# Agent attention with a gated FFN: the score passes regrouped by row half, one finished column per block

## The chip, the cores and the metric

One core of a Trainium2 chip runs the kernel; the other cores are idle. The metric is the device time of one execution in microseconds (us). Three executions of the kernel before took 1880.52, 1881.68 and 1882.74 us, median 1881.68 us. One further execution was profiled and took 1880.13 us.

## The reference

For four batches of 12480 tokens with 128 channels and 49 agents per batch, cut to what matters:

```python
a2k     = softmax(scale * agents @ k.T)        # 49 x 12480, per batch
agent_v = a2k @ v                              # 49 x 128
q2a     = softmax(scale * q @ agents.T)        # 12480 x 49
x       = q2a @ agent_v                        # 12480 x 128
h       = x @ w_in                             # 128 -> 2048
out     = (h * sigmoid(1.702 * h)) @ w_out     # 2048 -> 128
```

The scores `agents @ k.T` and `q @ agents.T` are what the change is about. The FFN on 49920 tokens is the bulk of the arithmetic.

## The kernel before

**The array in halves.** TensorE works as two row halves: a matmul takes 64 rows of its operands (rows 0 to 63 for half 0, 64 to 127 for half 1), and a matmul of half 0 and one of half 1 run side by side, each into a PSUM bank of its own. The FFN does this in `up` (bank `ph`) and `down` (bank pair `po`) through the helper `on_rows`, so line 119 stands for all these matmuls. An operand in full precision is kept as a high and a low part, and three products (high by high, high by low, low by high) make one. The low part `gl` of an activation is made on VectorE by `low` (line 611), from `g` and its high part `gh`; `gh` comes from a DMA that converts, or from a cast on ScalarE (line 605).

**Groups.** One key group is 8 blocks of 120 tokens, one query group 8 blocks of 128 tokens. A group's tile has channels on the partitions and tokens along the row. `split` takes it apart into three bf16 parts x0, x1, x2 by four pieces on VectorE: pieces 0 and 1 (line 228, then 230) make x1 and x2 of the first half of the columns, pieces 2 and 3 those of the second half. x0 is the upper half of each word and needs no work.

**Scores.** `scores` takes the eight blocks in turn. Channels 0 to 63 lie on row half 0 and channels 64 to 127 on row half 1, so each half computes a partial score of the same block by six bf16 products, and half k leaves its partial sum in bank k of a pair `ps_m`. Eight blocks, six products, two halves: 96 matmuls a group (line 243). `score_sum` adds the two partial sums: ScalarE copies bank 0 to SBUF (line 255), and VectorE adds bank 1 to the copy (line 256). For keys the sum goes to `score`. For queries it goes to `e_sb`, and `query_shift` then takes the maximum over the agents (line 528) and subtracts it (line 529). There are 39 key groups (batches 1 to 3; batch 0 goes another way at the start, through `first_scores`) and 49 query groups.

**Order.** The order on every engine is written out by hand: a step counter t advances by two, each pair of steps does `up`, `low`, `high` and `down` for two feature tiles, and a table `at[t]` says which attention job goes into which step. The keys of batch 1 are placed by `K_FIRST` every four steps (13 groups, some 100 to 240 us into the span); those of batches 2 and 3 by `K_AT`, at wider spacing. The bank pair of scores, of the query transposes and of the key-value products is one buffer (`ps_m`, one at a time), so a user of the pair waits until the one before has been read out. VectorE, ScalarE and TensorE each take their instructions strictly in the order written.

**Loads.** A key group comes by one DMA on the SyncE queue (line 261), 13 steps ahead, into one of three buffers; the agents come by one DMA at the very start (line 122), ahead of the first queries (line 519).

Of the kernel before, what the change touches and what calls it, by code (L numbers as in the profile page):

```python
# [8 lines left out]
F32 = mybir.dt.float32  # L9
F32R = mybir.dt.float32r  # L10
BF16 = mybir.dt.bfloat16
# [4 lines left out]
ALU = mybir.AluOpType  # L16
AX = mybir.AxisListType

P = 128
TB = 120  # L20
KB = 8
KG = TB * KB
QB = 128
CH = 512
# [25 lines left out]
def kernel(  # L50
# [10 lines left out]
    nc = tc.nc  # L61
    B, C, N = qT.shape
    A = agT.shape[2]
# [6 lines left out]
    H = P // 2  # L70
# [33 lines left out]
    def two_banks():  # L104
        return turns[1].tile([P, 2, 512], F32, name="ps_m", tag="pair")
# [94 lines left out]
    ag_part = odd.tile([P, B, 3, A], BF16, name="ag_part")  # L200

    def split_agents():
        rest = ag_sb
        for i in range(3):
            nc.vector.tensor_copy(out=ag_part[:, :, i, :], in_=rest)
            if i < 2:
                ag_rest = work.tile([P, B, A], F32, name="ag_rest")
                nc.vector.tensor_sub(out=ag_rest, in0=rest, in1=ag_part[:, :, i, :])
                rest = ag_rest

    def halves(t):
# [21 lines left out]

    def scores(parts, places, ps=None):
        x0, x1, x2 = parts
        ps = bank_pair(ps)
        products = [(x0, 0), (x0, 1), (x0, 2), (x1, 0), (x1, 1), (x2, 0)]
        for j, parts in enumerate(places):
            for b, t0, o, n in parts:
                for i, (x, y) in enumerate(products):  # L240
                    for k in range(2):
                        r = rows(k)
                        nc.tensor.matmul(  # L243
                            out=ps[k][o : o + n, j * A : (j + 1) * A],
                            lhsT=x[r, t0 : t0 + n],
                            rhs=ag_part[r, b, y, :],
                            start=(i == 0),
                            stop=(i == len(products) - 1),
                            tile_position=(k * H, o),
                        )  # L250
# [12 lines left out]

    def first_keys(g):
# [247 lines left out]
    def query_load(n):  # L512
        t = loads.tile([P, GT], F32, name="qt", tag="qt", bufs=1)
        for c in range(2):
            m = 2 * n + c
            for lo in range(0, CH, width(m)):
                for b, i, j in spans(m * CH, width(m)):
                    t0 = m * CH + i - b * N
                    nc.sync.dma_start(
                        out=t[:, c * CH + lo + i : c * CH + lo + j], in_=qT[b, :, t0 : t0 + j - i]  # L520
                    )
        return t

    def query_shift(ps):
        sd = e_sb[:QB, :, 0:A]
        score_sum(ps, QB, sd)
        m = work.tile([P, KB], F32, name="m")
        nc.vector.tensor_reduce(out=m[:QB], in_=sd, axis=AX.X, op=ALU.max)
        nc.vector.tensor_tensor(
            out=sd, in0=sd, in1=m[:QB].unsqueeze(2).broadcast_to([QB, KB, A]), op=ALU.subtract  # L530
        )
        return sd

# [147 lines left out]
            pieces[n](i)  # L681

    def do_key_scores(b, g):
        banks[b, g] = scores(k_parts.pop((b, g)), [[(b, j * TB, 0, P)] for j in range(KB)])
# [12 lines left out]
    def do_query_scores(n, ps=None):  # L697
        if n < NG:
            places = []
            for j in range(KB):  # L700
                m = 2 * n + j * 2 // KB
                t0 = m * CH + j * QB % CH % width(m)
                places.append([(b, j * QB + lo, lo, hi - lo) for b, lo, hi in spans(t0, QB)])
            banks[n] = scores(q_parts.pop(n), places, ps)

    def do_query_shift(n):
# [36 lines left out]
    with tc.manual_schedule(engines={E.PE, E.Activation, E.DVE, E.Pool, E.SP}):  # L743
# [7 lines left out]
        nc.vector.tensor_copy(out=ag_0[:, 0:A], in_=ag_sb[:, 0, :])  # L751
        split_agents()
        for c in range(2):
            nc.vector.tensor_add(
# [284 lines left out]
```

## Time and profile before

| what | value |
|---|---|
| median of three executions | 1881.68 us |
| the profiled execution's own time | 1880.13 us |
| its span | 1878.4 us |
| TensorE matmul busy | 1852.3 us (99%) |
| VectorE busy | 1535.7 us (82%) |
| ScalarE busy | 1491.5 us (79%) |
| mean granted TensorE clock | 0.999 |

Busy time of TensorE is read with care: matmuls are pipelined, and the end of each is modelled, so a short pause may be hidden by the modelled end of the matmul before it. The span is 1.73 us shorter than the execution's own time, and that execution is 1.55 us below the median.

### The profile page before, as it was taken

The numbers are of one execution on the slowest core, as the hardware profiler recorded it, in microseconds if no ns is written. First come the engines' busy times: TensorE is split into PE (matmuls) and PEld (weight loads), VectorE is DVE, ScalarE is ACT, GpSimd is POOL, SyncE is SP. The second block draws the span as 40 slices with busy tenths as digits, with TensorE's granted clock in tenths as the row PEclk, the third lists the DMA queues.
The fourth block names the chain that finished last, engine by engine and source line by source line (L and its number), as shares of the span: only waits on it lengthen the run. The fifth ranks groups of instructions, "written<-read, shape, count | busy, mean of one in ns | idle before, by whom it ended". The sixth has DMA issues, their size and how long they took to land.

```text
span 1878.4 us, 56411 instructions
## 1 busy us (share of the span) xinstructions
PE 1852.3 (99%) x24100; PEld 1714.4 (91%) x24100; DVE 1535.7 (82%) x1978; ACT 1491.5 (79%) x2410; POOL 332.5 (18%) x591
## 2 busy tenths in 40 slices
PE   7999999999999999999999999999999999999999
PEld 4678889998899999899889999999989999999998
DVE  7888999888789899888778998998877677777765
ACT  3677787887778777888887877878878888888886
POOL 1111111111111111121111111111111121211111
PEclk9999999999999999999999999999999999999999
DMA  9577777777577777777757777777666666666665
GB/s 360 186 225 216 210 209 213 217 211 223 166 206 225 212 213 221 206 210 218 216 170 217 215 212 219 215 214 210 196 180 186 196 198 197 206 199 198 198 191 148
DMA packets 138108, 390.99 MB, mean 208 GB/s; under 512 B 16825, under 2 KB 18489, under 8 KB 137857
## 3 DMA queue, kind: packets, MB, share of 16 engines
q0 software_dynamic: 77776, 255.10, 47.6%
q1 hardware_dynamic: 60081, 132.29, 22.9%
q8 instruction: 189, 3.10, 0.7%
q14 instruction: 62, 0.51, 0.1%
HBM read 81.53 MB, written 50.99 MB: 71 GB/s over the span
## 4 chain that ended last, share of the span: by engine, by line
PE 88%; DVE 5%; DMA 3%; issue 2%; ACT 2%; SPq 0%; POOL 0%; POOLq 0%; DVEq 0%; ACTq 0%
PE po L119 53%; PE ph L119 26%; PE ps_m L243 5%; PE ps_m L119 2%; DVE gl L611 2%; DMA kt<-kT 1%; DMA gh<-g 1%; ACT g L593 1%; DVE rest L228 1%; PE ps_m L505 1%; DVE rest L230 1%; PE ps_m L559 1%; DMA outT<-o 1%; DMA words<-w_out 0%; PE ph L284 0%
## 5 line engine op out<-in xcount | busy, mean ns | idle before, releaser
L593 ACT ACTIVATE g<-ph 128x512 f32<-128x512 f32 x1568 | 807.8, 603 | 275.6 <-PE ph L119 263.7
L611 DVE TENSOR_TENSOR gl<-g,gh 128x1024 fp32r<-128x1024 f32 x776 | 922.1, 1213 | 73.6 <-ACT gh L605 51.6
L119 PE MATMUL po<-gh,wo_h 64*128 64x512 f32 (+1 forms) x3104 | 548.0, 395 | 0.1
L119 PE MATMUL po<-gl,wo_h 64*128 64x512 f32 (+1 forms) x3104 | 535.6, 387 | 3.1 <-DVE gl L611 2.8
L119 PE MATMUL po<-gh,wo_l 64*128 64x512 f32 (+1 forms) x3104 | 533.3, 386 | 0.0
L603 POOL DMA_DIRECT2D gh<-g x436 | 236.5, 544 | 1371.0 <-ACT g L593 1067.2
L119 PEld LDWEIGHTS po<-gl,wo_h 64*128 64x128 f32 x3104 | 365.1, 184 | 22.5 <-DVE gl L611 9.7
L119 PEld LDWEIGHTS po<-gh,wo_l 64*128 64x128 f32 x3104 | 367.0, 184 | 14.2 <-issue 0.2
L119 PE MATMUL ph<-hi,wh 64*128 64x512 f32 (+4 forms) x1616 | 373.8, 384 | 0.3 <-DVE wl L509 0.3
L119 PE MATMUL ph<-hi,wl 64*128 64x512 f32 (+4 forms) x1616 | 371.6, 381 | 0.0
L119 PE MATMUL ph<-lo,wh 64*128 64x512 f32 (+4 forms) x1616 | 370.8, 380 | 0.4 <-DMA lo<-lo 0.4
L605 ACT CAST gh<-g 128x1024 fp32r<-128x1024 f32 (+1 forms) x340 | 357.6, 1053 | 9.0
L119 PEld LDWEIGHTS po<-gh,wo_h 64*128 64x128 f32 x3104 | 348.5, 185 | 15.8 <-issue 4.6
L119 PEld LDWEIGHTS ph<-hi,wh 64*128 64x128 f32 x1616 | 208.2, 184 | 14.5 <-ACT g L593 5.7
L119 PEld LDWEIGHTS ph<-lo,wh 64*128 64x128 f32 x1616 | 208.5, 184 | 8.9 <-DMA lo<-lo 0.8
L119 PEld LDWEIGHTS ph<-hi,wl 64*128 64x128 f32 x1616 | 206.5, 184 | 7.2 <-issue 0.7
L638 ACT COPY o<-po 128x1024 f32<-128x1024 f32 x97 | 98.4, 1014 | 56.6 <-PE po L119 55.9
L230 DVE TENSOR_TENSOR rest<-rest 128x512 bf16<-128x512 f32 (+2 forms) x176 | 129.2, 741 | 0.9
L243 PE MATMUL ps_m<-ag_part,rest 64*128 64x49 bf16 x4188 | 119.8, 181 | 0.3 <-DVE rest L230 0.3
L243 PEld LDWEIGHTS <-rest 64*128 64x128 bf16 (+1 forms) x4236 | 112.3, 93 | 0.8 <-DVE rest L230 0.4
L644 POOL DMA_DIRECT2D outT<-o x97 | 85.3, 880 | 96.4 <-DMA outT<-o 70.2
L256 DVE TENSOR_TENSOR e_sb<-ps_m,e_sb 128x392 f32<-128x392 f32 x48 | 27.1, 565 | 89.5 <-ACT e_sb L255 89.5
(143 smaller groups left out, 1322.0 us busy)
## 6 DMA issues: line engine op xcount, KB each, us to landing
gh<-g POOLq DMA_DIRECT2D x434, 512.0 KB, 3.5
kt<-kT SPq DMA_DIRECT2D x52, 480.0 KB, 5.0
outT<-o SPq DMA_DIRECT2D x97, 256.0 KB, 2.0
outT<-o POOLq DMA_DIRECT2D x97, 256.0 KB, 4.2
qt<-qT SPq DMA_DIRECT2D x94, 256.0 KB, 4.9
vt<-v SPq DMA_DIRECT2D x39, 480.0 KB, 4.9
hi<-hi SPq DMA_DIRECT2D x96, 128.0 KB, 2.8
lo<-lo SPq DMA_DIRECT2D x96, 128.0 KB, 2.4
```

Source lines behind the costliest of these rows:

```text
L119: nc.tensor.matmul(out=out, lhsT=lhsT[r], rhs=rhs[r], start=start, stop=stop, tile_position=(k * H, 0))
L228: nc.vector.tensor_sub(out=r[:, s], in0=t[:, s], in1=halves(t)[0][:, s])
L230: nc.vector.tensor_sub(out=halves(r)[1][:, s], in0=r[:, s], in1=halves(r)[0][:, s])
L243: nc.tensor.matmul(out=ps[k][o : o + n, j * A : (j + 1) * A], lhsT=x[r, t0 : t0 + n], rhs=ag_part[r, b, y, :], start=(i == 0), stop=(i == ...
L256: nc.vector.tensor_add(out=out, in0=h[1], in1=out)
L505: nc.tensor.matmul(out=pw[:, i * 256 : i * 256 + m], lhsT=w["avT"], rhs=w_in_sb[:, t : t + m], start=True, stop=True)
L593: nc.scalar.activation(out=g[:, k, :n], in_=ph[k][:, :n], func=AF.Gelu_apprx_sigmoid)
L603: nc.gpsimd.dma_start(out=gh, in_=g)
L605: nc.scalar.copy(out=gh, in_=g)
L611: nc.vector.tensor_sub(out=gl, in0=g, in1=gh.bitcast(F32))
L638: nc.scalar.copy(out=o, in_=po[:, :, :n])
L644: nc.gpsimd.dma_start(out=outT[:, m * CH : m * CH + width(m)], in_=o[:, 1], accum_op=ALU.add)
```

## The change

Each row half gets four blocks of its own (half 0 blocks 0 to 3, half 1 blocks 4 to 7) and takes both channel halves of them in turn, six products each. So twelve products accumulate into one column range, and a score is finished in PSUM; nothing is left to add. For that the tiles are laid out otherwise: rows 0 to 63 hold the first four blocks, with channels 0 to 63 in the first half of the columns and channels 64 to 127 in the second; rows 64 to 127 hold the last four blocks in the same way. The agents are kept twice, once on each row half.

The score copy of a key group is one ScalarE instruction, and the addition is gone. A query group has neither copy nor addition: the maximum and the subtraction read PSUM. A key load is two DMAs of 64 partitions, and so is the load of the agents; the query loads stay two DMAs, each of 64 partitions now. The core of the diff:

```diff
-    ag_sb = odd.tile([P, B, A], F32, name="ag_sb")
-    nc.sync.dma_start(out=ag_sb, in_=agT)
+    ag_sb = lines.tile([P, 2, B, A], F32, name="ag_sb", tag="o", bufs=1)
+    for k in range(2):
+        nc.sync.dma_start(out=ag_sb[rows(k)], in_=agT.rearrange("(h p) b a -> p h b a", h=2))
...
     def scores(parts, places, ps=None):
         x0, x1, x2 = parts
-        ps = bank_pair(ps)
-        products = [(x0, 0), (x0, 1), (x0, 2), (x1, 0), (x1, 1), (x2, 0)]
-        for j, parts in enumerate(places):
-            for b, t0, o, n in parts:
-                for i, (x, y) in enumerate(products):
+        ps = two_banks() if ps is None else ps
+        products = [(h, x, y) for h in range(2) for x, y in ((x0, 0), (x0, 1), (x0, 2), (x1, 0), (x1, 1), (x2, 0))]
+        half = KB // 2
+        for j in range(half):
+            blocks = [places[j], places[half + j]]
+            for piece in range(max(len(x) for x in blocks)):
+                for i, (h, x, y) in enumerate(products):
                     for k in range(2):
...
+                                out=ps[o : o + n, k, j * A : (j + 1) * A],
+                                lhsT=x[rows(k), h * half * t0[1] + t0[0] : h * half * t0[1] + t0[0] + n],
+                                rhs=ag_part[rows(k), h, b, y, :],
...
-    def score_sum(ps, n, out):
-        h = [ps[k][:n, : KB * A].rearrange("p (j a) -> p j a", a=A) for k in range(2)]
-        nc.scalar.copy(out=out, in_=h[0])
-        nc.vector.tensor_add(out=out, in0=h[1], in1=out)
+    def blocks_of(ps, n):
+        return ps[:n, :, : KB // 2 * A].rearrange("p k (j a) -> p k j a", a=A)
...
     def key_load(b, g):
         t = loads.tile([P, KG + PAD], F32, name="kt", tag="kv")
-        nc.sync.dma_start(out=t[:, 0:KG], in_=kT[b, :, g * KB : (g + 1) * KB, :].rearrange("p j t -> p (j t)"))
+        for k in range(2):
+            j = g * KB + k * KB // 2
+            nc.sync.dma_start(
+                out=t[rows(k), 0:KG].rearrange("p (h x) -> p h x", h=2),
+                in_=kT[b, :, j : j + KB // 2, :].rearrange("(h p) j t -> p h (j t)", h=2),
+            )
...
     def query_shift(ps):
+        s = blocks_of(ps, QB)
         sd = e_sb[:QB, :, 0:A]
-        score_sum(ps, QB, sd)
         m = work.tile([P, KB], F32, name="m")
-        nc.vector.tensor_reduce(out=m[:QB], in_=sd, axis=AX.X, op=ALU.max)
+        mk = m[:QB].rearrange("p (k j) -> p k j", k=2)
+        nc.vector.tensor_reduce(out=mk, in_=s, axis=AX.X, op=ALU.max)
...
     def do_key_store(b, g):
-        score_sum(banks.pop((b, g)), TB, score[:TB, g * KB : (g + 1) * KB, :])
+        out = score[:TB, g * KB : (g + 1) * KB, :].rearrange("p (k j) a -> p k j a", k=2)
+        nc.scalar.copy(out=out, in_=blocks_of(banks.pop((b, g)), TB))
```

Besides, the split of the agents into three bf16 parts (`split_agents`) runs over 392 elements a row instead of 196, and the agents of batch 0 are copied by two instructions of 64 partitions.

Two places show how the order moves. The first is VectorE among the keys of batch 1, before; each row is a line of the kernel, an operation, output and inputs, the output's size and in brackets the engines it waits for. `kt` is a key tile, `rest` the low parts of a split, `score` and `e_sb` the scores of keys and queries, `gl` the low part of an activation:

```order
L256 TENSOR_TENSOR e_sb<-ps_m,e_sb 128x8x49 [waits Activation_49]
L528 TENSOR_REDUCE m<-e_sb 128x8 [waits DVE_49]
L529 TENSOR_TENSOR e_sb<-e_sb,m 128x8x49 [waits DVE_49]
L611 TENSOR_TENSOR gl<-g,gh 128x1024
L256 TENSOR_TENSOR score<-ps_m,score 120x392 [waits Activation_49]
L228 TENSOR_TENSOR rest<-kt 128x488 [waits DMAHW4_49]
L611 TENSOR_TENSOR gl<-g,gh 128x1024 [waits DMASW7_49]
L414 TENSOR_TENSOR run_max<-score,run_max 120x392 [waits DVE_49]
```

The same place in the changed kernel, whose line numbers are higher by 1 to 12:

```order
L537 TENSOR_REDUCE m<-ps_m 128x8 [waits PE_49]
L538 TENSOR_TENSOR e_sb<-ps_m,m 128x8x49 [waits DVE_49]
L623 TENSOR_TENSOR gl<-g,gh 128x1024 [waits Activation_49]
L229 TENSOR_TENSOR rest<-kt 128x488 [waits DMAHW1_49,DMAHW0_49]
L623 TENSOR_TENSOR gl<-g,gh 128x1024 [waits DMASW7_49,PE_49]
L421 TENSOR_TENSOR run_max<-score,run_max 120x392 [waits Activation_49]
```

Both additions (line 256) are gone; the query's maximum waits for TensorE instead of ScalarE, and the wait for ScalarE's copy of the key scores has moved behind the split and the next low part, to the running maximum.

The second place is the SyncE queue at the same stretch, before; `hi` and `lo` are parts of the weights of a query group, which change row halves there:

```order
L261 DMA kt<-kT 128x960 [waits DMAHW4_49,DVE_49,PE_49]
L577 DMA hi_1663<-hi 64x512 [waits DMASW1_49,DMAHW5_49,DMASW0_49,Activation_49]
L577 DMA hi_1663<-hi 64x512 [waits DMAHW6_49]
L577 DMA lo_1664<-lo 64x512 [waits DMASW3_49,DMAHW7_49,DMASW2_49,DVE_49]
L577 DMA lo_1664<-lo 64x512 [waits DMAHW0_49]
L261 DMA kt<-kT 128x960 [waits DMAHW1_49,DVE_49,PE_49]
```

And in the changed kernel:

```order
L265 DMA kt<-kT 64x2x480 [waits DMAHW0_49,DVE_49,PE_49]
L265 DMA kt<-kT 64x2x480 [waits DMAHW1_49]
L589 DMA hi_1662<-hi 64x512 [waits DMASW1_49,DMAHW2_49,DMASW0_49,Activation_49]
L589 DMA hi_1662<-hi 64x512 [waits DMAHW3_49]
L589 DMA lo_1663<-lo 64x512 [waits DMASW3_49,DMAHW4_49,DMASW2_49,DVE_49]
L589 DMA lo_1663<-lo 64x512 [waits DMAHW5_49]
L265 DMA kt<-kT 64x2x480 [waits DMAHW6_49,DVE_49,PE_49]
L265 DMA kt<-kT 64x2x480 [waits DMAHW7_49]
```

One issue more stands in the queue for every key group, ahead of what follows it; the order is otherwise the same.

## Rows read from the trace of the kernel before

**Rows 1.** The page's first lines: span, busy time and instructions of each engine.

```profile
span 1878.4 us, 56411 instructions
PE 1852.3 (99%) x24100; PEld 1714.4 (91%) x24100; DVE 1535.7 (82%) x1978; ACT 1491.5 (79%) x2410; POOL 332.5 (18%) x591
```

**Rows 2.** Busy time by stretch: columns as in the head row.

```profile
core 0: us, PE busy (x) PEld busy (x) DVE busy (x) ACT busy (x) POOL busy (x), PEclk, DMA share, GB/s
6.00:50.00 44.00, 36.91 (x402) 22.99 (x404) 32.63 (x72) 19.04 (x45) 2.38 (x4) 0.96 1.02 388
...
100.00:240.00 140.00, 134.21 (x2530) 116.72 (x2527) 127.51 (x176) 105.34 (x170) 22.93 (x48) 1.00 0.73 214
...
400.00:1850.00 1450.00, 1449.24 (x18598) 1371.01 (x18596) 1176.31 (x1456) 1185.45 (x1893) 263.65 (x460) 1.00 0.71 205
```

**Rows 3.** Waits in 100 to 240 us: in total, times, longest.

```profile
DVE score L256 <- ACT score L255: 11.4, 4, 3.3
...
PE po L119 <- DVE gl L611: 2.6, 4, 1.0
PE ps_m L243 <- DVE e_sb L256: 2.4, 3, 1.2
```

**Rows 4.** Timeline of VectorE around a late key copy: start, us, instruction, idle before.

```profile
141.20 0.57 DVE L545 TENSOR_TENSOR p_pad<-e_sb,z 128x392 f32<-128x392 f32 x1
145.05 0.56 DVE L256 TENSOR_TENSOR score<-ps_m,score 120x392 f32<-120x392 f32 x1 [3.28 <-ACT score L255]
145.53 0.66 DVE L228 TENSOR_TENSOR rest<-kt 128x488 f32<-128x488 f32 x1
146.11 2.35 DVE L611 TENSOR_TENSOR gl<-g,gh 128x1024 fp32r<-128x1024 f32 x2
```

**Rows 5.** Timeline of GpSimd's queue and of TensorE, the same moment.

```profile
138.62 0.53 POOL L603 DMA_DIRECT2D gh<-g  x1 [0.44 <-DVE rest L228]
...
147.38 0.73 PE L119 MATMUL po<-gl,wo_h 64*128 64x512 f32 x4 [0.52 <-DVE gl L611]
```

**Rows 6.** Timeline of VectorE and TensorE up to a wait for the bank pair.

```profile
112.97 0.57 DVE L256 TENSOR_TENSOR score<-ps_m,score 120x392 f32<-120x392 f32 x1 [1.81 <-ACT score L255]
...
129.54 0.39 PE L119 MATMUL ph<-hi,wl 64*128 64x512 f32 x2
...
129.77 0.39 PE L119 MATMUL ph<-lo,wh 64*128 64x512 f32 x2
...
130.75 0.55 DVE L256 TENSOR_TENSOR e_sb<-ps_m,e_sb 128x392 f32<-128x392 f32 x1
...
131.35 0.25 PE L243 MATMUL ps_m<-ag_part,kt 64*128 64x49 bf16 x6 [1.20 <-DVE e_sb L256]
```

**Rows 7.** Groups of instructions by line: busy us, mean ns, idle before, releaser.

```profile
L529 DVE TENSOR_TENSOR e_sb<-e_sb,m 128x392 f32<-128x392 f32 x49 | 27.8, 567 | 1.7
...
L256 DVE TENSOR_TENSOR e_sb<-ps_m,e_sb 128x392 f32<-128x392 f32 x48 | 27.1, 565 | 89.5 <-ACT e_sb L255 89.5
...
L256 DVE TENSOR_TENSOR score<-ps_m,score 120x392 f32<-120x392 f32 x39 | 22.0, 563 | 45.3 <-ACT score L255 45.2
...
L297 DVE TENSOR_REDUCE first_mx<-ph 128x1 f32<-128x480 f32 x12 | 7.5, 652 | 4.9 <-PE ph L284 4.9
```

**Rows 8.** Timeline of VectorE and TensorE: a key split that ends inside its score group.

```profile
151.16 0.25 PE L243 MATMUL ps_m<-ag_part,kt 64*128 64x49 bf16 x6
151.25 0.23 PE L243 MATMUL ps_m<-ag_part,rest 64*128 64x49 bf16 x6
151.29 0.73 DVE L230 TENSOR_TENSOR rest<-rest 128x480 bf16<-128x480 f32 x1
```

**Rows 9.** Timeline of SyncE at the start, and one key load later.

```profile
0.75 0.39 SPq L122 DMA_DIRECT2D ag_sb<-agT  x1
...
120.51 0.34 SPq L261 DMA_DIRECT2D kt<-kT  x1
```

**Rows 10.** The page's DMA issues: count, KB each, median us to landing.

```profile
kt<-kT SPq DMA_DIRECT2D x52, 480.0 KB, 5.0
```

More of the change, by code (lines that the diff above doesn't have):

```diff
@@ L198, in down_weights_low @@
         nc.vector.tensor_sub(out=wo_l[:, s, :], in0=wo, in1=wo_h[:, s, :].bitcast(F32))
-    ag_part = odd.tile([P, B, 3, A], BF16, name="ag_part")
+    ag_part = odd.tile([P, 2, B, 3, A], BF16, name="ag_part")
     def split_agents():
@@ L204, in split_agents @@
         for i in range(3):
-            nc.vector.tensor_copy(out=ag_part[:, :, i, :], in_=rest)
+            nc.vector.tensor_copy(out=ag_part[:, :, :, i, :], in_=rest)
             if i < 2:
-                ag_rest = work.tile([P, B, A], F32, name="ag_rest")
-                nc.vector.tensor_sub(out=ag_rest, in0=rest, in1=ag_part[:, :, i, :])
+                ag_rest = lines.tile([P, 2, B, A], F32, name="ag_rest", tag="rest")
+                nc.vector.tensor_sub(out=ag_rest, in0=rest, in1=ag_part[:, :, :, i, :])
                 rest = ag_rest
@@ L235, in scores @@
         x0, x1, x2 = parts
-        ps = bank_pair(ps)
-        products = [(x0, 0), (x0, 1), (x0, 2), (x1, 0), (x1, 1), (x2, 0)]
-        for j, parts in enumerate(places):
-            for b, t0, o, n in parts:
-                for i, (x, y) in enumerate(products):
-                    for k in range(2):
[L242 to L250, printed above, removed]
@@ L251, in scores @@
-        return ps
-    def score_sum(ps, n, out):
-        h = [ps[k][:n, : KB * A].rearrange("p (j a) -> p j a", a=A) for k in range(2)]
-        nc.scalar.copy(out=out, in_=h[0])
-        nc.vector.tensor_add(out=out, in0=h[1], in1=out)
+        ps = two_banks() if ps is None else ps
[5 more added lines that the diff above has]
+                for i, (h, x, y) in enumerate(products):
+                    for k in range(2):
+                        if piece < len(blocks[k]):
+                            b, t0, o, n = blocks[k][piece]
+                            nc.tensor.matmul(
+                                out=ps[o : o + n, k, j * A : (j + 1) * A],
+                                lhsT=x[rows(k), h * half * t0[1] + t0[0] : h * half * t0[1] + t0[0] + n],
+                                rhs=ag_part[rows(k), h, b, y, :],
+                                start=(i == 0),
+                                stop=(i == len(products) - 1),
+                                tile_position=(k * H, o),
+                            )
@@ L259, in key_load @@
+        return ps
+    def blocks_of(ps, n):
+        return ps[:n, :, : KB // 2 * A].rearrange("p k (j a) -> p k j a", a=A)
     def key_load(b, g):
         t = loads.tile([P, KG + PAD], F32, name="kt", tag="kv")
[L261 removed]
+        for k in range(2):
[3 more added lines that the diff above has]
+                in_=kT[b, :, j : j + KB // 2, :].rearrange("(h p) j t -> p h (j t)", h=2),
+            )
@@ L519, in query_load @@
                     nc.sync.dma_start(
-                        out=t[:, c * CH + lo + i : c * CH + lo + j], in_=qT[b, :, t0 : t0 + j - i]
+                        out=t[rows(c)].rearrange("p (h x) -> p h x", h=2)[:, :, lo + i : lo + j],
+                        in_=qT[b, :, t0 : t0 + j - i].rearrange("(h p) t -> p h t", h=2),
                     )
@@ L524, in query_shift @@
     def query_shift(ps):
+        s = blocks_of(ps, QB)
         sd = e_sb[:QB, :, 0:A]
-        score_sum(ps, QB, sd)
         m = work.tile([P, KB], F32, name="m")
-        nc.vector.tensor_reduce(out=m[:QB], in_=sd, axis=AX.X, op=ALU.max)
+        mk = m[:QB].rearrange("p (k j) -> p k j", k=2)
+        nc.vector.tensor_reduce(out=mk, in_=s, axis=AX.X, op=ALU.max)
         nc.vector.tensor_tensor(
-            out=sd, in0=sd, in1=m[:QB].unsqueeze(2).broadcast_to([QB, KB, A]), op=ALU.subtract
+            out=sd.rearrange("p (k j) a -> p k j a", k=2),
+            in0=s,
+            in1=mk.unsqueeze(3).broadcast_to([QB, 2, KB // 2, A]),
+            op=ALU.subtract,
         )
@@ L683, in do_key_scores @@
     def do_key_scores(b, g):
-        banks[b, g] = scores(k_parts.pop((b, g)), [[(b, j * TB, 0, P)] for j in range(KB)])
+        places = [[(b, (j % (KB // 2) * TB, TB), 0, P)] for j in range(KB)]
+        banks[b, g] = scores(k_parts.pop((b, g)), places)
     def do_key_store(b, g):
-        score_sum(banks.pop((b, g)), TB, score[:TB, g * KB : (g + 1) * KB, :])
+        out = score[:TB, g * KB : (g + 1) * KB, :].rearrange("p (k j) a -> p k j a", k=2)
+        nc.scalar.copy(out=out, in_=blocks_of(banks.pop((b, g)), TB))
     def do_key_values(b, g):
@@ L702, in do_query_scores @@
                 t0 = m * CH + j * QB % CH % width(m)
-                places.append([(b, j * QB + lo, lo, hi - lo) for b, lo, hi in spans(t0, QB)])
+                at0 = j % (KB // 2) * QB
+                places.append([(b, (at0 + lo, QB), lo, hi - lo) for b, lo, hi in spans(t0, QB)])
             banks[n] = scores(q_parts.pop(n), places, ps)
@@ L750 @@
         nc.vector.memset(sel, 0.0)
-        nc.vector.tensor_copy(out=ag_0[:, 0:A], in_=ag_sb[:, 0, :])
+        for k in range(2):
+            nc.vector.tensor_copy(out=ag_0[rows(k), 0:A], in_=ag_sb[rows(k), k, 0, :])
         split_agents()
```

## The prediction

> **What bounds the kernel now.** I read the page's first lines, then the busy time by stretch, then the waits of the stretch that shows idle time, then the timeline at its worst places. TensorE is busy for 1852.3 of 1878.4 us [rows 1], so no other engine's relief can give back more than 26 us. The table by stretch says where these lie [rows 2]. From 400 to 1850 us TensorE idles 1450.00 - 1449.24 = 0.76 us: there it alone is the bound, and VectorE, at 1176 of 1450, has time to spare. From 6 to 50 us the share of the DMA engines is 1.02: the first loads set the pace, whatever the engines do. Between them, from 100 to 240 us, lie the 13 key groups of batch 1. There TensorE idles 140.00 - 134.21 = 5.79 us and VectorE is busy for 127.51 us, 91%, the highest share of any long stretch. The waits of that stretch name two causes that make up 5.0 of the 5.79 us [rows 3]: four waits for `gl`, the low part of an activation (2.6 us), and three score groups that wait until VectorE has emptied the bank pair of a query group before them (2.4 us).
>
> **What lies behind those waits.** VectorE has finished at 141.77 (141.20 + 0.57), and then stands until 145.05 because the next row in its order is the addition of a key group, which needs ScalarE's copy: 3.28 us [rows 4]. The split and two `gl` queue behind it. The `gh` that the first `gl` needs was sent off at 138.62 [rows 5], so it could have been made before 144; it starts at 146.11, and TensorE waits until 147.38 [rows 5]. Four such waits for ScalarE add up to 11.4 us [rows 3]. The other kind: TensorE comes to a key group at about 130.0, but the addition of the query group before it, which frees the bank pair, ends at 130.75 + 0.55, and the group starts at 131.35 [rows 6]. VectorE had worked without a pause until then.
>
> The idle column understates both. The matmuls before the second wait start 0.23 us apart (129.54, 129.77), the next one 1.58 us later [rows 6]: 1.35 us are lost where 1.20 are shown, since the modelled end covers 0.15. Over some nine waits this makes 5.79 + 9 x 0.15, about 7.1 us, and that is all that VectorE's relief can return in this stretch.
>
> **The change, part by part.**
>
> TensorE's scores: 96 matmuls a group before and after, the same shapes, two halves side by side in two banks, each weight load as before. I cost them at nothing. The price of being wrong follows from the pace of the passes: six start within 0.09 us (151.16 to 151.25, [rows 8]), so 96 take about 1.4 us and 88 groups about 125 us, and each per cent on a pass is 1.25 us, either way.
>
> Key groups: 39 additions of 563 ns go from VectorE, with 45.3 us of waiting for the copy [rows 7]. The copy stays, and frees the bank pair by its own end, without the addition's 0.56 us. The running maximum takes over the wait for the copy, but stands behind the split and the next `gl`, so these go on; its own input is long there when its turn comes.
>
> Query groups: 48 additions of 565 ns in the pair `ps_m` (and one at the start), with 89.5 us of waiting, and as many ScalarE copies go [rows 7]. The maximum and the subtraction now read PSUM. No row shows this subtraction from PSUM; the nearest are the addition with one input in PSUM, 565 ns, and the one wholly in SBUF, 567 ns, for the same 392 elements, and for the maximum the first batch's, 652 ns for 480 elements in PSUM [rows 7]. So I take 0.57 us each, between 0.56 and 0.65. What is dearer is the release: the pair used to be free after one instruction, now after two, 0.57 us later in VectorE's order.
>
> [...]
>
> VectorE in the stretch: 13 key additions and 4 query additions, 17 x 0.56 = 9.5 us less work, of 127.5, and the 11.4 us of pauses may be used. By the time of the wait at 131.35 it is ahead by the pause of 1.81 us before the addition at 112.97, by that addition and by the next key group's, 0.57 each [rows 6], together near 2.9 us; the later release takes 0.57 of it, and the 1.35 us that TensorE lost are covered. The waits for `gl` go too, except the first, which stands behind a query's maximum and subtraction and keeps about half of its 1.0 us. I leave 0.6 us there and 0.6 us for remains at the three bank waits: 7.1 - 1.2 = 5.9 us come back. Nothing comes back from 400 to 1850 us, since 0.76 us is all that idles.
>
> The splits: a group's first block now needs both halves of the columns, so the last piece is due at the twelfth pair instead of the thirtieth; at 0.03 us a pair that is 0.3 us into the group instead of 0.85. In [rows 8] the piece ends at 152.02, 0.86 us into its group: just in time before, and 0.55 us late now, if VectorE were no earlier. With 2 us and more of lead it is there. I cost it at nothing, and at most at 0.55 us for each of four such groups, 2.2 us.
>
> Loads: one issue more for each of 39 key groups, 0.34 us on the queue [rows 9]. Behind it stand the exchanges of `hi` and `lo` and the output stores, none of which TensorE waits for in this stretch [rows 3]. The load issued at 120.51 lands some 5.0 us later [rows 10], and the split that reads it begins at 145.53 [rows 4], 20 us after that; even a landing twice as long is covered. At the very start the agents' second DMA stands ahead of the queries and first keys: 0.39 us [rows 9], before the DMA engines are loaded, so nothing hides it. I take +0.4 us, between 0 and twice that. The agents' split grows by some 1.2 us on VectorE, under the first loads; the query shift there is shorter by a copy and an addition, which the load-bound stretch swallows.
>
> Sum against the profiled execution: 1880.13 - 5.9 + 0.4 = 1874.6 us. That execution is 1.55 us below the median of the three, so for the median 1881.7 - 5.5 = 1876.2 us, 0.29% less.
>
> **Rivals.**
>
> *VectorE's time comes back as another wait.* TensorE runs closer to VectorE and ScalarE, and `gl` then waits for `gh` or for ScalarE's cast instead of for the addition. For it: `gh` takes its way over a DMA or over ScalarE, whose copies of key scores come as late as before (they still cost 3.28 us after the work before, [rows 4]). Against it: the `gh` of [rows 5] was there early. Half of 5.9 would return: 1881.7 - 3.0 + 0.4 = 1879.1 us, within 0.2%.
>
> *The pair is held longer, and the split comes late.* If VectorE's lead is used up (its order has the splits and `gl` in the same places, and its inputs come from TensorE), each bank wait grows by 0.57 us and the four late pieces cost 0.55 us each: 3 x 0.57 + 4 x 0.55 + 0.4 = 4.3 us and nothing gained, 1886.0 us. It decides where VectorE reaches a query's maximum less than 0.57 us earlier than it reached the addition. Against it: 17 instructions fewer.
>
> *The change doesn't relieve anything that counts,* since TensorE is the bound almost everywhere: only the start shows, 1882.1 us. Against it stand the 5.0 us of waits that name the lines removed or the `gl` right behind them.
>
> *More than predicted:* everything lost comes back, the start's 0.4 is swallowed by the loads, and a little from the rest: 1881.7 - 7.1 - 0.8 = 1873.8 us.
>
> **How the numbers follow.** Forecast 0.57 (with a spread of about 1.5 us, so a seventh of it within 0.2%), another wait 0.22, nothing relieved 0.07, held longer 0.07, more 0.07. About 0.2%, 3.8 us, is what a measurement of this kernel can tell from no change. Faster by more than that: six sevenths of the forecast, 0.49, all of the last, 0.07, and a quarter of the second, 0.05, make 0.61. Slower by more: the held pair, and a little for dearer score passes, 0.09. The same: 0.30. The range for 8 in 10 reaches from the last case to just past no change: 1873.0 to 1882.5 us.
>
> **What would show it.** Right: from 100 to 240 us TensorE's idle time falls from 5.79 to some 1 us, the rows of line 256 and their waits are missing, score groups no longer wait for a query's shift, VectorE's share there falls to about 84% although the stretch is shorter, and the stretch from 400 us on is as long as before. The maximum and subtraction read 0.56 to 0.57 us. Wrong: a score group whose 96 passes take longer than 1.4 us; a wait of a score group for line 231 or 538; a split that waits for a key load; a first matmul that starts more than 0.5 us later than before.

## The result, and the profile after

The changed kernel takes 1892.3 us (median of four runs, 1891.35 to 1892.92) against 1882.2 for the kernel before, measured beside it: ratio 1.0055, 95% interval 1.0043 to 1.0068. It is 10 us slower, where 1876.2 us was forecast. The profiled execution is one of the four (1891.35 us). Its first lines, answering [rows 1]:

```profile
span 1889.6 us, 56486 instructions
PE 1863.0 (99%) x24100; PEld 1728.0 (91%) x24100; DVE 1494.4 (79%) x1891; ACT 1471.1 (78%) x2361; POOL 333.1 (18%) x591
```

VectorE has 41 us less to do (the additions of [rows 7] had 49 us, but instructions that follow one another overlap a little, by 0.08 us at 145.53 in [rows 4]), and TensorE has 10.7 us more with as many instructions. The same three stretches as [rows 2], the same columns:

```profile
6.00:50.00 44.00, 35.79 (x386) 21.13 (x386) 32.77 (x74) 17.15 (x44) 2.53 (x4) 0.96 1.02 371
...
100.00:240.00 140.00, 138.55 (x2658) 123.39 (x2655) 124.76 (x165) 107.02 (x173) 25.77 (x54) 1.00 0.83 223
400.00:1850.00 1450.00, 1448.75 (x18510) 1372.59 (x18508) 1139.88 (x1387) 1163.66 (x1844) 261.21 (x457) 1.00 0.72 203
```

TensorE's idle time among the keys of batch 1 fell from 5.79 to 1.45 us, and the waits of that stretch [rows 3] are smaller:

```profile
PE ps_m L247 <- DVE e_sb L538: 1.1, 3, 0.4
PE po L119 <- DVE gl L623: 0.4, 1, 0.4
```

What was meant to happen did, though the first of these rows is a wait that the prediction named as a sign of being wrong (see below). To find what else happened, take a landmark that both kernels have, the first matmul of each score group (line 243 before, 247 after), and subtract the times. This lag compares one profiled execution of each kernel and is worked out from the traces. It is 0.09 us at the very first group and then, with the time in the kernel before as head row:

```
                     68.6  250.1  475.3  516.2  1385.2  1426.1  1806.0
changed kernel       6.28   0.50   1.48   6.24    7.19   11.60   11.43
```

Four numbers tell the story: 6.3 us are lost at the start, 5.8 come back by 250 us, and 4.8 and 4.4 are lost at two single query groups. The remaining 1.8 us creep in between.

**The two groups.** A batch has 12480 tokens, 97.5 blocks of 128, so one block in group 12 and one in group 36 belong half to one batch and half to the next, and are taken as two pieces of 64 tokens. Before, both row halves took the same block, so both ran pieces of 64. After, its partner on the other half is a whole block. Either way these two groups have 108 passes (a pass is one matmul of `scores`) and not the 96 that the section on the kernel before gives for every group. TensorE in the first of these groups after, then before:

```profile
477.30 0.87 PE L247 MATMUL ps_m<-ag_part,qt 64*64 64x49 bf16 x6
478.10 0.87 PE L247 MATMUL ps_m<-ag_part,rest 64*64 64x49 bf16 x6
478.90 0.87 PE L247 MATMUL ps_m<-ag_part,qt 64*64 64x49 bf16 x6
479.70 0.87 PE L247 MATMUL ps_m<-ag_part,rest 64*64 64x49 bf16 x6
480.50 0.27 PE L247 MATMUL ps_m<-ag_part,qt 64*64 64x49 bf16 x3
...
480.99 0.25 PE L247 MATMUL ps_m<-ag_part,qt 64*128 64x49 bf16 x6
481.09 0.23 PE L247 MATMUL ps_m<-ag_part,rest 64*128 64x49 bf16 x6
```

```profile
475.86 0.25 PE L243 MATMUL ps_m<-ag_part,rest 64*64 64x49 bf16 x6
476.05 0.25 PE L243 MATMUL ps_m<-ag_part,qt 64*128 64x49 bf16 x6
476.14 0.23 PE L243 MATMUL ps_m<-ag_part,rest 64*128 64x49 bf16 x6
```

Read the start times: six passes usually start within 0.08 to 0.1 us, but these take 0.80, 0.13 each, for 24 passes. In these four rows, which put passes of both shapes together, 64x64 on one half and 64x128 on the other take turns, as the code orders them. From its first pass to its last the group takes 4.80 us instead of 1.62. Behind it the granted clock is 0.50 for 3.4 us; before, it stayed at 1.00 (after, then before 1.5 us earlier, which is the lag ahead of the group):

```profile
481.60:485.00 3.40, 3.40 (x31) 2.75 (x24) 2.26 (x3) 0.00 (x0) 0.00 (x0) 0.50 0.37 90
```

```profile
480.10:483.50 3.40, 3.40 (x30) 2.73 (x28) 2.01 (x5) 2.79 (x5) 0.98 (x2) 1.00 0.43 160
```

So 4.76 us = 3.18 in the passes + 1.58 behind them. The other group, at 1392 us, is alike: 4.41 us = 3.19 + 1.22.

**The start.** The queue's first rows, answering [rows 9]:

```profile
0.74 1.41 SPq L123 DMA_DIRECT2D ag_sb<-agT  x2
2.19 1.26 SPq L526 DMA_DIRECT2D qt<-qT  x2
3.49 0.59 SPq L273 DMA_DIRECT2D kt<-kT  x1
```

A DMA of 64 partitions with two pieces each took 0.63 to 0.70 us to issue here, where the one of the agents took 0.39, and the first keys follow at 3.49 instead of 2.12 us. Later the second query group's load stands in front of the output weights `words`, in both kernels. The chain of work that ended last shows how late these come, after and then before (start, us, what):

```profile
42.38 12.36 DMA words<-w_out
57.14 3.78 PE ph L512 x6
```

```profile
41.63 8.89 DMA words<-w_out
52.62 2.00 PE ph L505 x6
```

0.75 us later issue, 3.47 us longer on the way, 1.78 us more for six matmuls at the lower clock, 0.50 from 57.14 to 60.92 us against 1.00 before: 6.0 of the 6.28. That clock is not the same in each execution: two kernels below, same_pieces and half_by_half, have the very same start; their lag at 68.6 us is 8.03 and 4.63 us, and in the second the clock doesn't fall there (its mean over the span is 1.000). So the start costs 4.6 to 8.0 us, and a difference of a microsecond or two between the lags of two executions says little. What the DMA engines moved in half-microsecond slices from 40 to 60 us, after and then before, shows why the weights were late:

```profile
GB/s 421 386 428 409 401 410 418 410 401 410 418 410 401 385 184 188 160 242 217 213 254 213 246 197 287 393 393 410 336 262 139 57 41 8 0 0 0 0 0 0
```

```profile
GB/s 395 399 418 410 410 410 418 410 401 410 406 389 401 397 389 438 377 422 393 401 385 270 123 123 49 0 0 0 0 0 0 0 0 0 0 139 262 254 258 361
```

From 47 us on the rate is about half for 5 us, some 210 GB/s against 410, although the same view shows the DMA engines busy for 90% and more of that time. In that stretch lie the 256 packets of 2 KB of the query load, now written to 64 partitions by each DMA; they take 160 ns on average instead of 87.

### The profile page after: what moved, and what is told of

Same layout as the page of the kernel before. It is cut to its first block, busy times and chain, and to the rows that moved or that the text cites. A ratio compares the mean times of both kernels' runs of the same rounds, so it can differ in the third digit from the quotient of the medians.

```text
span 1889.6 us, 56486 instructions
## 1 busy us (share of the span) xinstructions
PE 1863.0 (99%) x24100; PEld 1728.0 (91%) x24100; DVE 1494.4 (79%) x1891; ACT 1471.1 (78%) x2361; POOL 333.1 (18%) x591
## 4 chain that ended last, share of the span: by engine, by line
PE 88%; DMA 5%; DVE 4%; issue 2%; ACT 1%; POOL 0%; SPq 0%; POOLq 0%; DVEq 0%; ACTq 0%
PE po L119 53%; PE ph L119 26%; PE ps_m L247 5%; PE ps_m L119 2%; DVE gl L623 2%; DMA gh<-g 2%; DMA kt<-kT 1%; PE ps_m L512 1%; DMA words<-w_out 1%; DVE rest L231 1%; DMA vt<-v 1%; DVE rest L229 1%; ACT g L605 1%; DMA outT<-o 1%; PE ps_m L571 0%
## 5 line engine op out<-in xcount | busy, mean ns | idle before, releaser
L623 DVE TENSOR_TENSOR gl<-g,gh 128x1024 fp32r<-128x1024 f32 x776 | 925.3, 1214 | 142.2 <-DMA gh<-g 80.5
L119 PE MATMUL po<-gh,wo_l 64*128 64x512 f32 (+1 forms) x3104 | 527.9, 386 | 0.0
L119 PE MATMUL ph<-hi,wh 64*128 64x512 f32 (+4 forms) x1616 | 366.6, 384 | 0.0
L119 PE MATMUL ph<-hi,wl 64*128 64x512 f32 (+4 forms) x1616 | 364.2, 381 | 0.0
L119 PE MATMUL ph<-lo,wh 64*128 64x512 f32 (+4 forms) x1616 | 362.7, 380 | 0.0
L119 PEld LDWEIGHTS po<-gh,wo_h 64*128 64x128 f32 x3104 | 343.8, 185 | 17.0 <-issue 4.8
L119 PEld LDWEIGHTS ph<-hi,wh 64*128 64x128 f32 x1616 | 201.6, 184 | 14.1 <-ACT g L605 5.5
L119 PEld LDWEIGHTS ph<-lo,wh 64*128 64x128 f32 x1616 | 201.8, 184 | 7.3
L119 PEld LDWEIGHTS ph<-hi,wl 64*128 64x128 f32 x1616 | 200.0, 184 | 6.5 <-issue 0.6
L247 PEld LDWEIGHTS <-qt 64*128 64x128 bf16 (+1 forms) x2364 | 64.8, 94 | 12.9 <-issue 11.7
```

What stands on the lines that cost most here:

```text
L247: nc.tensor.matmul(out=ps[o : o + n, k, j * A : (j + 1) * A], lhsT=x[rows(k), h * half * t0[1] + t0[0] : h * half * t0[1] + t0[0] + n], rh ...
L623: nc.vector.tensor_sub(out=gl, in0=g, in1=gh.bitcast(F32))
```

## Experiments on the two groups

**same_pieces**: both row halves use one shape.

```diff
+            if len(blocks[0]) != len(blocks[1]):
+                cuts = max(blocks, key=len)
+                blocks = [
+                    x if len(x) == len(cuts) else [(x[0][0], (x[0][1][0] + o, x[0][1][1]), o, n) for _, _, o, n in cuts]
+                    for x in blocks
+                ]
```

> The changed kernel, but in the two query groups that cross a batch boundary the partner block is cut at the same place as the crossing block, so that both row halves always run tiles of one shape (120 passes in these groups instead of 108). Theory A (passes of a 64-token tile on one half and a 128-token tile on the other, taken in turn, cost 0.13 us each; and the slow stretch drops TensorE's clock for 3.4 us behind it): the two groups take 1.4 to 1.6 us instead of 4.80, the clock stays at 1.00 behind them, 2 x 4.6 = 9 us come back: 1883 us. Rival B (it is not the turns: passes of 64 tokens, or passes with no partner on the other half, are slow themselves): half the tiles are still of 64 tokens, the groups take 4.8 us or more, 1892 us.

1884.3 us (10 runs, 1881.64 to 1888.55), ratio to before 1.0015 [1.0005, 1.0024]. The groups take 1.88 and 1.70 us, a little more than expected, and the clock stays up behind them. 8.0 us are back, with more passes than in the changed kernel.

**half_by_half**: the same passes as in the changed kernel, in another order.

```diff
+            mixed = len(blocks[0]) != len(blocks[1])
+            for only in (0, 1) if mixed else (None,):
...
-                        if piece < len(blocks[k]):
+                            if piece < len(blocks[k]) and only in (None, k):
```

> The changed kernel, but where a crossing block meets a whole one, half 0 takes all its passes first and then half 1, so no two shapes are taken in turn; all 36 of these passes run without a partner. Theory A (turns of shape): 24 + 12 passes at 0.03 to 0.04 us, some 1.3 us for them, the group near 2.1 us, no fall of the clock, 2 x 4.2 = 8.4 us come back: 1884 us. Rival B (passes without a partner are what is slow; before the chip was asked, the 12 unpaired ones of 64 tokens are seen at 0.04 us): the groups stay at 4.8 us or grow, 1892 us or more.

1883.3 us (10 runs), ratio 1.0006 [0.9996, 1.0015]; groups of 2.15 and 2.11 us, no fall of the clock. Passes without a partner are cheap here, 2.1 us a group; taking turns is not, at 4.80 in the changed kernel.

**before_cuts**: the suspected cost put into the kernel before, alone.

```diff
+CUT = {20: "mixed", 22: "apart", 24: "same", 28: "mixed", 30: "apart", 32: "same"}
...
+            if cut and j in (1, 2):
+                (b, t0, o, n), = parts
+                two = [(b, t0, o, H), (b, t0 + H, o + H, H)]
+                blocks = [two if cut == "same" else parts, two]
```

> The kernel before, with two blocks cut into 64 and 64 tokens in six ordinary query groups: in groups 20 and 28 on half 1 alone and taken in turn with the whole block of half 0 (mixed), in groups 22 and 30 the same passes but half by half (apart), in groups 24 and 32 on both halves (same). Theory A: the mixed groups take 1.22 + 24 x 0.13 = 4.3 us and cost 4.6 us with the clock behind them, the others 1.4 to 2.1 us at full clock; in all 1882.2 + 2 x 4.6 + 2 x 0.7 + 2 x 0.2 = 1893.2 us. Rival B (unpaired passes): the groups apart are at least as dear as the mixed ones. Rival C (the new layout makes it slow: one column range written from both channel halves, twelve products long): mixed groups here, with six products into a bank of their half, stay under 2 us, 1884 us.

1894.7 us, ratio 1.0064 [1.0049, 1.0079], 13 us slower with two blocks cut in each of six groups. Groups mixed: 5.07 and 4.50 us; apart: 2.20 and 2.24; same: 1.68 and 1.64. A mixed group, then one apart (the last pass of a row and the first of the next can start together):

```profile
785.53 0.74 PE L252 MATMUL ps_m<-ag_part,qt 64*64 64x49 bf16 x5
786.20 0.87 PE L252 MATMUL ps_m<-ag_part,rest 64*128 64x49 bf16 x6
786.86 0.27 PE L252 MATMUL ps_m<-ag_part,qt 64*64 64x49 bf16 x3
...
863.88 0.25 PE L252 MATMUL ps_m<-ag_part,qt 64*128 64x49 bf16 x3
863.97 0.23 PE L252 MATMUL ps_m<-ag_part,rest 64*128 64x49 bf16 x3
```

The layout is not at fault, nor the number of passes: the turns of shape are, at 0.13 us a pass. The clock fell inside the first mixed group (six of its last passes start within 0.125 us, where 0.08 is usual) and not at the second, so that part of the price is not certain each time. Five of the kernels here have two groups with such turns each (the changed one, this one, late_q1, wide_q1, wide_all). Of the ten, four cost 2.9 to 3.3 us of lag with no fall of the clock, four 4.4 to 4.8 us with 3.4 us at the lower clock, two about 6 us with 6.8 us of it. Between 70 us and the last 5 us of the span no kernel here shows the lower clock anywhere else.

## Experiments on the start

**late_q1**: in the list of loads, `"v12 q1 w4 w5"` becomes `"v12 w4 w5 q1"`.

> The changed kernel with the second query group's load issued behind the first two loads of output weights instead of ahead of them; the load is needed some 20 us later, near 70 us. Theory A (at the start: the query load, now written to 64 partitions at a time, moves at some 230 GB/s instead of 400 and the weights stand behind it, TensorE waits and its clock falls): the weights land 4 to 5 us earlier, no clock at 0.50 between 55 and 62 us, 3 to 5 of the 6.3 us lost at the start come back: 1888 us. Rival D (the queue starts 1.4 us later because the issues ahead of the first keys take longer, and all of the start is load-bound from there): at most the 1.8 us of the two issues that go from ahead of the weights, 1890.5 us or more.

1888.6 us (6 runs), ratio 1.0033 [1.0020, 1.0045]: 3.7 us back, lag at 68.6 us 2.15 instead of 6.28, no lower clock from 55 to 62 us. Rival D allowed 1.8 us.

**wide_q1**: that one load in the old form, `out=t[:, c * CH + lo + i : ...], in_=qT[b, :, ...]` for `n == 1`.

> The changed kernel with one load in the old form: the second query group's two DMAs write 128 partitions with one piece of 2 KB each, instead of 64 partitions with two pieces; bytes, pieces and place in the queue are the same (the scores of that one group are then made from values in the wrong places). Theory A (writing 64 partitions at a time is what is slow): its 2 KB packets take some 87 ns instead of 160, the weights behind it land 2 to 3.5 us earlier, and the start loses 2 to 4 us instead of 6.3: 1889 us. Rival D (the queue's later start alone): the packets are as slow, the weights land at most 0.3 us earlier, 1892 us.

1890.8 us (four runs), 1.0047 [1.0034, 1.0061]. The packets take 87 ns again and the lag at 68.6 us is 3.05. From 40 to 60 us the rate no longer breaks down:

```profile
GB/s 401 404 418 404 430 415 409 393 401 410 418 401 418 406 389 393 406 426 393 397 401 397 447 352 238 139 123 107 49 16 0 0 0 0 0 0 0 0 0 0
```

The six matmuls behind the weights start earlier and at full clock (1.00 from 54 to 58 us, where the changed kernel has 0.61):

```profile
55.69 2.00 PE ph L512 x6
```

The whole time moved by only 1.5 us, between the 3.3 of Theory A and the nothing of Rival D: in the profiled execution the lag grows by 0.8 us more than the changed kernel's from 250 to 475 us, and by 2.1 us more from 516 to 1385 us, which this experiment doesn't explain.

**before_narrow_q1**: the same thing put into the kernel before.

```diff
+        if n == 1:
+            for r in (rows(0), rows(1)):
+                nc.sync.dma_start(
+                    out=t[r].rearrange("p (c x) -> p c x", c=2),
+                    in_=qT[0, r, GT : 2 * GT].rearrange("p (c x) -> p c x", c=2),
+                )
+            return t
```

> The kernel before with the second query group's load alone written to 64 partitions at a time (two DMAs, as many bytes, values in the right places). Theory A: the weights behind it land 1.2 to 3.5 us later and TensorE, idle for longer, may fall to its lower clock: 1.2 to 5 us more, 1883 to 1887 us, and packets slower than 87 ns per 2 KB. Rival D: 1881.8 us, and packets as fast as before.

1885.8 us (10 runs), 1.0022 [1.0013, 1.0031]: 4 us slower by one load. The weights take longer, and the matmuls behind them meet the lower clock (0.68 on average from 54 to 58 us):

```profile
42.59 11.37 DMA words<-w_out
56.21 3.28 PE ph L505 x6
```

Its lag is 4.84 us at 68.6 us and 4.95 at 250.1: a late start alone gave nothing back later. The 5.8 us of the changed kernel are therefore its own. The source rows joined to packets of 4 KB here, so their time isn't compared.

**wide_all**: all query and key loads in the old form.

> The changed kernel with all query and key loads in the old form, 128 partitions at a time, one DMA for a key group (all scores are then made from values in the wrong places; the agents still come by two DMAs). Theory A: the start loses only what the agents' second issue costs, about 1 us instead of 6.3, and nothing changes from 250 us on, where no load is waited for: 1892.3 - 5 = 1887 us. Rival E (narrow loads also cost in the steady part, by slowing the gh transfers that share the DMA engines): the stretch from 250 to 470 us gets back its 1 us and batches 2 and 3 theirs too, 1885 us or less. Rival D: 1891 us.

1888.7 us (6 runs, 1885.53 to 1890.86), 1.0038 [1.0026, 1.0050]; lag 3.43 us at 68.6, where Theory A expected about 1. From 250 to 475 us it loses 0.9 us, as the changed kernel does (1.0), so narrow loads cost nothing there, and Rival E falls.

**before_late**: the first key load held back by three tiny loads; **fixed_late_pairs** and **fixed_early** are built on `fixed` (below).

```diff
+    for i in range(3):
+        nc.sync.dma_start(out=spare[:, i, :], in_=agT[:, 0, 0:4])
```

> The kernel before with three tiny loads (2 KB each, read by nobody) put into the queue behind the agents, so that the first key load is issued some 1.2 us later, as in the changed kernel. Theory D (the rest of the loss at the start is this later issue, carried through a load-bound stretch): the first query group behind the start, at 68.6 us before, comes 1.2 to 3 us later, 1883.5 to 1885 us. Theory H (the rest comes from the query exchange, which the shorter query shift lets go earlier, among the key loads): the issue alone costs under 0.5 us there, 1882.3 us.

1882.8 us (11 runs), 1.0006 [0.9997, 1.0015]; lag 1.59 us at 68.6 us. The time lies between Theory D and Theory H and is not clear of the kernel before. By size, a later first key load could be about half of the 2.0 to 3.4 us that stay in the kernels with this query load repaired and no additions. That is argued and not shown: here the lag is 1.67 us from the very first score group on, where the changed kernels are late by only 0.1 to 1.1 us.

**fixed_early**: the first key load issued ahead of the agents. **before_early**: that and the late second query load, in the kernel before.

> The version with both repairs, with the first key load issued ahead of the agents and the first queries. Theory A (what is left of the loss at the start, 2.8 us, is that the DMA engines get their first large load at 3.5 us instead of 2.1): the engines are busy 2 us earlier, and 2 to 3 us come back: 1880 to 1881 us. Rival G (the agents and queries, now behind a key load, land later and hold up the first scores): no gain, 1883 us or more.

> The kernel before with the two orders of loads alone: the first key load ahead of the agents, and the second query load behind two loads of output weights. If that order is worth something by itself, 1 to 2 us less than before, 1880 us; if only the narrow loads make it count, 1881.7 us.

1881.1 us, 0.9996 [0.9987, 1.0005], and 1882.2 us, 1.0002 [0.9993, 1.0011]. Theory A's time came out, but its mechanism isn't seen: the lag of fixed_early at 68.6 us is still 2.99 (`fixed` 2.76), and the intervals of the two overlap. The orders are worth nothing to the kernel before.

**fixed_late_pairs**: `if p == 1` becomes `if p == 2` for the first query group's pairs.

> The version with both repairs, with the first query group's transposes and the exchange of its hi and lo parts one stage of the start later (some 7 us). Theory H: the key load issued at 22.2 us no longer shares the DMA engines with the exchange, TensorE doesn't wait 3.5 us for it at 32 to 36 us and its clock stays up, 1.5 to 3 us come back: 1880 to 1881.5 us. Theory D: nothing, 1883 us.

1881.4 us, 0.9999 [0.9990, 1.0008]; lag 2.72 us. The time is Theory H's, but not by its way: the clock doesn't stay up. It is at 0.50 from 22.9 and from 40.0 us, for 3.4 us each, where `fixed` has one such stretch of 6.8 us from 34.6 us. What a full clock would give back here is not tested by this, and a gain at the start is not shown.

## Experiments on the gain, and the mended kernel

**fixed**: same_pieces and late_q1 together.

> The changed kernel with both repairs: the partner blocks cut like the crossing blocks, and the second query group's load behind the first two loads of output weights. Theory A, by what the two repairs gave one by one (8.0 and 3.7 us): 1892.3 - 8.0 - 3.7 = 1880.6 us, just under the kernel before (1881.8). If the two losses hide one another (a rival), 1883 us or more.

1882.9 us (11 runs, 1880.0 to 1884.9), 1.0005 [0.9996, 1.0013]. 9.4 us are back, not 11.7: the repairs don't quite add up, and the time is nearer to the rival's 1883 us than to Theory A's 1880.6.

**fixed_adds** and **fixed_key_adds**: VectorE's instructions put back, in the first behind both score copies, in the second behind the key groups' alone.

```diff
+        nc.scalar.copy(out=out, in_=s)
+        nc.vector.tensor_tensor(out=out, in0=s, in1=out, op=ALU.max)
```

> The version with both repairs (1882.9 us), with a VectorE instruction put back where each addition stood: it waits for ScalarE's copy, reads the same 392 elements from PSUM and the copy, and takes their maximum, which leaves the values as they are; for queries the maximum over the agents and the subtraction read SBUF again, as before. Theory A (the gain among the keys of batch 1 comes from these instructions and their waits being gone): the 6 to 7 us that this version gives back from 100 to 250 us are lost again, TensorE idles some 5.8 us from 100 to 240 us, 1889 us. Rival F (the gain comes from something else in the change, such as the bank pair being written in another order): it stays, 1883 us.

> The same, but only the key groups get their instruction back; the query groups keep the short way. If the waits of key additions for ScalarE (11.4 us on VectorE) are what cost, most of it is lost again: 1887 to 1888 us. If the query groups' copy, addition and late release are, 1884 us, and four of the six us stay.

1889.2 us, 1.0040 [1.0025, 1.0056], and 1891.9 us, 1.0055 [1.0041, 1.0069]. Between 68.6 and 250.1 us `fixed` gains 6.60 us; these two lose 1.85 and 3.03. The instruction of the key groups alone takes all of it. It takes more than that, 9.6 us of lag and 9 us of time where 4 to 5 were expected, so the kernel with it is worse there than the kernel before; why isn't shown. The other kernels bear out that the additions decide: the ten profiled executions without any addition gain 4.7 to 6.6 us in this stretch, 5.6 on average, and the four variants of the kernel before gain -0.1 to 0.3. The waits of fixed_key_adds from 100 to 240 us, VectorE's first:

```profile
DVE score L709 <- ACT score L708: 14.1, 7, 3.4
...
PE ps_m L253 <- DVE e_sb L544: 3.1, 3, 1.3
PE po L119 <- DVE gl L629: 2.8, 6, 0.6
PE ps_m L253 <- DVE rest L231: 1.3, 3, 0.5
```

In `fixed` TensorE's only one is the first of these, shorter:

```profile
PE ps_m L253 <- DVE e_sb L544: 1.2, 3, 0.4
```

**fixed_best**: fixed_late_pairs with the agents' second load issued by GpSimd.

> The same, and the second of the agents' two loads is issued by GpSimd, so that the first key load stands 0.7 us earlier in the SyncE queue. Theory D: 0.7 to 1.5 us less than the version before it. Theory H: as the version before it, within 0.5 us. Both repairs, D and H together would make it 1879.5 us, which would beat the kernel before.

1880.8 us (11 runs, 1878.8 to 1883.5), 0.9994 [0.9985, 1.0003]; lag 1.95 us at 68.6, and no lower clock at the start (its mean over the span is 1.000). The 0.6 us to fixed_late_pairs are not clear of the noise. It beats the changed kernel by some 11 us and is level with the kernel before.

## Why the prediction was wrong

*The dense stretch: right in mechanism and size.* 5.9 us forecast, 5.8 measured from 68.6 to 250.1 us. The key additions with their wait for ScalarE were the cause: with them put back the gain is gone. What the query additions do by themselves was not tried. VectorE's share there was to be 84% and is 89%; the 84% is 118 us of work over the old length of the stretch, over the shortened one it would have been 88%. One mark of being wrong did show: score groups wait for line 538, the query's subtraction, for 1.1 us where 0.6 were left. The rival that another wait takes over has its sign, too: the low part now stands idle for its `gh` DMA for 80.5 us in all, before for 18.7. In the steady part that hardly reaches TensorE, which idles 1.25 us from 400 to 1850 us instead of 0.76. The groups of [rows 7] and the low part over the whole span, after:

```profile
L538 DVE TENSOR_TENSOR e_sb<-ps_m,m 128x392 f32<-128x392 f32 x48 | 27.2, 567 | 1.6
L537 DVE TENSOR_REDUCE m<-ps_m 128x8 f32<-128x392 f32 x48 | 27.1, 566 | 45.8 <-PE ps_m L247 45.8
...
L623 DVE TENSOR_TENSOR gl<-g,gh 128x1024 fp32r<-128x1024 f32 x776 | 925.3, 1214 | 142.2 <-DMA gh<-g 80.5
```

Maximum and subtraction from PSUM take 566 and 567 ns, as forecast.

*"TensorE's scores: 96 matmuls a group before and after, the same shapes ... I cost them at nothing": the step that failed first.* It holds for 86 of 88 groups (1.22 to 1.33 us from first pass to last behind the start). The other two have 108 passes before and after. There the count stayed, but not the shapes that stand side by side, and the diff shows it: `if piece < len(blocks[k])` stands there because the two halves may have different numbers of pieces. I priced a pass and not a change of shape between passes. It cost 9.2 us by the lag; the repairs gave back 8 to 9. The mark named, "a score group whose 96 passes take longer than 1.4 us", points at the right line, but at the wrong groups.

*"At the very start ... I take +0.4 us, between 0 and twice that": the second step that failed.* One more issue was counted at 0.39 us; it was 1.37 us by the first key load, since the narrow issues were longer too, 0.63 to 0.70 us each where those of the agents and queries took 0.39 and 0.45. And the query loads "stay two DMAs", so I gave them no price, although each now writes half the partitions, in the one stretch where I had read a DMA share of 1.02 [rows 2]. That load alone is worth 3.2 us of lag by wide_q1, one execution against another, and slows the kernel before by 4 (before_narrow_q1, ten runs), which is the firmer number. For the key loads the cover that I named held.

*The release of the bank pair, "0.57 us later in VectorE's order": priced in the dense stretch alone.* It counts in the steady part as well. At three places a key-value product (`ps_m<-v_pair,e_pair`) stands right behind a query group and needs its bank pair. The first of them, after and then before:

```profile
292.12 0.57 DVE L538 TENSOR_TENSOR e_sb<-ps_m,m 128x392 f32<-128x392 f32 x1
292.31 0.41 PE L119 MATMUL ph<-lo,wh 64*128 64x512 f32 x2
292.83 1.22 PE L119 MATMUL ps_m<-v_pair,e_pair 64*128 64x258 f32 x16
```

```profile
291.05 0.56 DVE L256 TENSOR_TENSOR e_sb<-ps_m,e_sb 128x392 f32<-128x392 f32 x1
291.85 0.42 PE L119 MATMUL ph<-lo,wh 64*128 64x512 f32 x2
292.07 1.16 PE L119 MATMUL ps_m<-v_pair,e_pair 64*128 64x258 f32 x16
```

After, the product starts 0.52 us behind the matmuls ahead of it and right behind the subtraction; before, 0.22 us behind them, with the pair free since 291.61. This recurs near 754 and 1209 us. Every kernel here whose query shift reads PSUM has it at two or three of the three places, and none of the others has it, fixed_adds included. The stretches from these three groups to the next hold 1.3 of the 1.8 us that creep in, and 2.3 of the 4.5 us that `fixed` loses behind 250 us; how much of that is this wait and what follows from it was not tested.

*What stays open.* Of the lag at the start 2 to 3 us remain in every mended kernel; a later first key load may be about half (before_late 1.59). And mended kernels lose part of their lead again between 250 and 1806 us: `fixed` goes from -3.84 to 0.65. The three stretches just named hold about half of that loss. Kernels with before's scores do so too in part (before_early 2.6 us, before_narrow_q1 2.1, before_late none), single runs of one kernel lie up to 8 us apart (fixed_adds), and the profiled execution of the kernel before, from which every lag counts, is itself 1.55 us under its median. The rest has no one place that I found. This, too, keeps the mended kernel from 1876 us.

## What to carry to other kernels

When two halves of an array get work of their own, look for the steps at which their pieces differ in shape, count the turns there, and run each half's pieces in one block or cut both alike (2.15 and 1.88 us here, against 4.80 in turn). The query load that was split by partitions kept its bytes and its packets but lost half its rate (some 210 GB/s against 410); ask of each such load whether it lies in a stretch that the DMA engines bound. Where a buffer is released by a later instruction, look for every user that stands right behind, in the steady part too. A gain read from one stretch is only as good as the list of everything else that the diff touches.

## What the runs showed of the hardware

Passes of 64x128 and 64x64 taken in turn on the two row halves started 0.13 us apart, against 0.013 for one shape (six in 0.08 us). In six of ten groups with 24 of them the granted clock fell to 0.50, inside the group or behind it, for 3.4 or 6.8 us. The 2 KB packets of the second query group's load, written to 64 partitions at a time, took 139 to 160 ns on average (160 in the changed kernel) against 87 (the kernel before, wide_q1), with those of 4 KB from 40 to 60 us at 180 to 195 against 164 (wide_q1 and wide_all). A maximum over PSUM cost 566 ns, over SBUF 561, and a subtraction 567 from either.
